# Second head mixing on 64-column halves of TensorE, in a talking-heads attention with a bilinear feed-forward layer

## Chip, core and metric

The kernel runs on one core of one Trainium2 chip. The metric is the device time of one execution in microseconds (us); less is better. All tensors are float32.

## What is computed

```python
def _attn_ref(q, k, v, w_pre, w_post):          # batch 4, 12 heads, 448 positions, 64 per head
    scale = 1.0 / np.sqrt(q.shape[-1])
    scores = scale * np.matmul(q, k.transpose(0, 1, 3, 2))
    scores = np.einsum('bhij,hg->bgij', scores, w_pre)      # first head mixing
    scores = scores - np.max(scores, axis=-1, keepdims=True)
    attn = np.exp(scores)
    attn = attn / (np.sum(attn, axis=-1, keepdims=True) + 1e-09)
    attn = np.einsum('bhij,hg->bgij', attn, w_post)         # second head mixing
    return np.matmul(attn, v).astype(np.float32)

def _moe_ref(x, w_a, w_b, w_out):               # 1792 tokens, 768 wide, 1536 inside
    return ((x @ w_a) * (x @ w_b) @ w_out).astype(np.float32)
```

The reference feeds the attention's output, heads side by side, to the second function.

## The kernel before, in words

Queries are cut into chunks of 120, 120, 120 and 88 per batch, 16 chunks in all, and a chunk into units of 20 queries (`units`, 23 per batch, 92 in all; the last unit of a batch has 8). The loop over `s` (one step per unit) is a software pipeline written out by hand: `tc.manual_schedule()` means that the order in the program is the order on every engine.

In step `s` the program issues, in this order:

- `pace(s - 1)`: a small copy on GpSimd that waits for a row sum of the step before, so that GpSimd's later DMAs don't run ahead;
- `load_v`: pieces of v, issued from GpSimd. Those of batch 0 go out in steps 2 and 4, those of batch b+1 in steps 6 and on of batch b (`V_AT`);
- `premix(s)` (L270): the first head mixing, four small matmuls on four quarters of the array, into the two PSUM buffers of tag `m`;
- `evac_p` of unit s-2 (L314): ScalarE copies the second mixing's result from PSUM to `ptt`;
- `smax(s)` (L279, L280): VectorE's row maximum, then ScalarE's exponential with row sums;
- one `qk` (L233, with its copy by ScalarE on L234) of a chunk that is needed later; its copy writes one of two buffers `s`, so it waits until the gathers of the chunk two before have read that buffer;
- in some steps two `av` (L328), the product with v for a group of eight units;
- `norm(s)` (VectorE: the reciprocal of the sum goes into the small matrix `kr`);
- `postmix` of unit s-1 (L303), the second head mixing, which the change rewrites;
- any second `qk` of the step, and then `load_k`, `load_q` and `spread_q` for later chunks, all on GpSimd (`spread_q` is a copy that `qk` needs).

`gather(u)` (L250) runs three units ahead on SyncE's queue. It is four DMAs of 60 rows of scores, from the buffer `s` into tiles `sb` (four buffers each), so that one unit's rows stand on 60 partitions per five queries.

`postmix` takes a block of ten queries. The probabilities `an` (124 rows: five queries with 12 heads, twice) are the stationary operand, 112 keys at a time, and `kr` (124 x 120) is the moving one. The result has keys on partitions, and four slices of keys side by side:

```python
        for r in range(R):
            nc.tensor.matmul(pp[:, r, :, :n], lhsT=an[:m, r * P:(r + 1) * P], rhs=kr[:m, :, :n])
```

Every float32 matmul shows as two weight loads and two matmuls in the trace, so a unit of two blocks is 16 records of each on L303.

`av` multiplies with v: stationary is v of one head (112 keys x 64), and the two heads of a pair go to the two column halves of the array, to partitions 0 to 63 and 64 to 127 of one PSUM buffer:

```python
                nc.tensor.matmul(
                    xp[64 * e:64 * e + 64, p % 3, :n],
                    lhsT=vt[b, g][:, h % 6, r],
                    rhs=ptt[a][:P, r, h, :n],
```

After the attention come the feed-forward layer's first two products (`run_a`, `run_b`) and the last one (`run_o`). Their PSUM buffers are tags `m` and `p`. `mm3` is three matmuls for every product, since the operands are split in a high and a low part.

The functions that the diff touches, with the profile's line numbers:

Of the kernel before, what the change touches and what calls it, by code (L numbers as in the profile page):

```python
# [7 lines left out]
F32 = mybir.dt.float32  # L8
# [13 lines left out]
def talking_heads_bilinear_kernel(  # L22
# [11 lines left out]
    nc = tc.nc  # L34
    B, _, G, S = k.shape
# [10 lines left out]
    AVC = GU * QU  # L46
    R = 4
    P = S // R
    CW = KD * 128
    AH = 3  # L50
    AV_AT = (1, 1, 3, 3, 5, 5)
# [56 lines left out]
    mask = const.tile([128, QB], F32, name="mask")  # L108
    wp = const.tile([128, 64], F32, name="wp")
    p2 = const.tile([128, 1], F32, name="p2")  # L110

    def ps_t():
        return ps.tile([128, 2, 512], F32, tag="t", name="pst", bufs=1)[:, 0]
# [71 lines left out]

    def load_v(b, i):

        g, e = divmod(i, 3)
        if e == 0:
            vt[b, g] = v_p.tile([P, H // 2, R, D], F32, tag=f"v{g}", name="v")  # L190
        nc.gpsimd.dma_start(out=vt[b, g][:, 2 * e:2 * e + 2], in_=v[b, g][:, 2 * e:2 * e + 2])

    def load_k(b, i):
        t = k_p.tile([128, S], F32, tag="k", name="k")
# [24 lines left out]
    def qk(c, i):  # L219
        b, t0, n = chunks[c]  # L220
        if c not in st:
            st[c] = big.tile([128, H, S], F32, tag="s", name="s")
        if c == 0 and i % 2:
            for g in range(2):
                rows = slice(D * g, D * g + D)
                sp = ps.tile([128, 512], F32, tag="mpx"[i // 2], name="psq")[:, :S]
                nc.tensor.matmul(sp[:n], lhsT=qt[c, i // QG][rows, i % QG], rhs=kt[b, i][rows])
                nc.vector.tensor_copy(st[c][:n, g * G + i], sp[:n])
            return
        sp = ps.tile([128, 2, 512], F32, tag="t", name="pst", bufs=1)[:, :, :S]  # L230
        for g in range(2):
            rows = slice(D * g, D * g + D)
            nc.tensor.matmul(sp[:n, g], lhsT=qt[c, i // QG][rows, i % QG], rhs=kt[b, i][rows])  # L233
        nc.scalar.copy(st[c].rearrange("p (g i) s -> p i g s", g=2)[:n, i], sp[:n])  # L234
# [58 lines left out]
        nc.vector.tensor_scalar(kr[:m], kf[:m], rc[:m], None, op0=ALU.mult)  # L293
        ant[u, j] = a, kr

    def postmix(k_):
        u, j, n = k_
        m = rows_of(n)
        pp = ps.tile([128, 512], F32, tag="p", name="pp")[:P, :R * H * QB]
        pp = pp.rearrange("p (r h t) -> p r h t", r=R, h=H)  # L300
        an, kr = ant.pop((u, j))
        for r in range(R):
            nc.tensor.matmul(pp[:, r, :, :n], lhsT=an[:m, r * P:(r + 1) * P], rhs=kr[:m, :, :n])  # L303
        pps[u, j] = pp

    def evac_p(k_):
        u, j, n = k_
        if (u, j) not in pps:
            return
        a = group_of[u]  # L310
        o = (u - groups[a][1]) * QU + j * QB
        if a not in ptt:
            ptt[a] = big.tile([128, R, H, AVC], F32, tag="pt", name="pt")
        nc.scalar.copy(ptt[a][:P, :, :, o:o + n], pps.pop((u, j))[:, :, :, :n])  # L314

    def av(a, p):
        b, u0, _ = groups[a]
        t0 = (u0 - b * NUB) * QU
        n = min(AVC, S - t0)
        g = p // 3  # L320
        if p % 3 == 0:
            xp = ps.tile([128, 512], F32, tag="x", name="xp")
            xps[g] = xp[:, :3 * AVC].rearrange("p (a t) -> p a t", a=3)
        xp = xps[g]
        for r in range(R):
            for e in range(2):
                h = 2 * p + e
                nc.tensor.matmul(  # L328
                    xp[64 * e:64 * e + 64, p % 3, :n],
                    lhsT=vt[b, g][:, h % 6, r],  # L330
                    rhs=ptt[a][:P, r, h, :n],
                    start=(r == 0),
                    stop=(r == R - 1),
                )
        if p % 3 == 2:
            xs = x_p.tile([128, 3, AVC], F32, tag="xs", name="xs")
            nc.vector.tensor_copy(xs[:, :, :n], xp[:, :, :n])
            later(lambda: nc.sync.dma_start(out=xd[b][:, 3 * g:3 * g + 3, t0:t0 + n], in_=xs[:, :, :n]), 1)
# [127 lines left out]
    def run_b(f, b):  # L466
        hh, ll = wt["f", f]
        x = xt[b]
        pb = (ps_t() if f == b == 0 else ps.tile([128, 512], F32, tag="p", name="pb"))[:, :S]
        mm3(pb, hh, ll, x[:, 0], x[:, 1], KD, KD)  # L470
        sa = sas.pop((f, b))
        hf = w_p.tile([128, S], F32, tag="an", name="hf", bufs=AB)
        nc.vector.tensor_tensor(hf, pb, sa, op=ALU.mult)
        later(lambda: nc.sync.dma_start(out=hd[b][:, f], in_=hf), 1)
# [15 lines left out]
    def run_o(j):  # L490
        b, m = divmod(j, KD)
        hh, ll = wt.pop(("o", j))
        th, tl = ht[b]
        po = ps.tile([128, 512], F32, tag="mp"[j % 2], name="po")[:, :S]
        mm3(po, hh, ll, th, tl, KF)
        so = sb_p.tile([128, S], F32, tag="sb1", name="so")
        nc.scalar.copy(so, po)
# [55 lines left out]
    with tc.manual_schedule():  # L553
# [19 lines left out]
            qk(0, i)  # L573
        spread_q(1, 0)
        setup_w()
        nxt_g = AH + 1
        for u in range(nxt_g):
            gather(u)
# [3 lines left out]
        for s in range(NU + 2):  # L582
# [14 lines left out]
                nxt_g += 1  # L597
            pace(s - 1)
            if s in (2, 4):
                for i in range(3):  # L600
                    load_v(0, 3 * (s // 2 - 1) + i)
            b, i = divmod(s, NUB)
            if b + 1 < B and 0 <= i - V_AT < 6:
                load_v(b + 1, i - V_AT)
            for fn in todo_at.pop(s, ()):
                fn()
# [13 lines left out]
                for k_ in blocks_of(s):  # L620
                    norm(k_)
            if 0 <= s - 1 < NU:
                for k_ in blocks_of(s - 1):
                    postmix(k_)
            for it in pairs[1:]:
                it[0](*it[1:])
            for it in after.get(s, ()):
# [130 lines left out]
```

## Time and profile before

| | |
|---|---|
| time, median of 3 runs | 990.07 us (985.38 to 995.18) |
| span of the profiled execution, first to last instruction | 991.0 us |
| TensorE with a matmul in flight | 963.7 us, 97% of the span |
| VectorE, ScalarE, GpSimd busy | 52%, 42%, 30% |
| attention | to about 466 us; the feed-forward layer from there |
| granted TensorE clock, mean | 0.989 of full speed |

The profiled execution has no separate time of its own; its span of 991.0 us lies 0.9 us above the median and inside the interval of the three runs. Matmuls are pipelined, so a busy TensorE says that something is in flight, not that the array is at its peak. The profile's matmul ends are modelled; the starts are not.

### The profile page before, as it was taken

To read this page: it belongs to the slowest core of one execution; us is meant where nothing else is said; L and a number is where in the kernel's file an instruction comes from. 1 tells how busy PE (TensorE), PEld (TensorE's weight loads), DVE (VectorE), ACT (ScalarE), POOL (GpSimd) and SP (SyncE) were. 2 spreads that over 40 slices of the span, in tenths; PEclk is the share of its full clock that TensorE was granted. 3 is DMA by queue.
4 is the path that set the end of the run, shared out by engine and by line. 5 is a ranking of instruction groups with operands and counts; after the bars stand their busy time and mean duration, and the time that the engine had idled before them with its cause. 6 is when DMAs were issued, how large, how long until landed. Compare 5 with 4: busy or idle time off the path is not lost.

```text
span 991.0 us, 17011 instructions
## 1 busy us (share of the span) xinstructions
PE 963.7 (97%) x6388; PEld 769.2 (78%) x6388; DVE 518.8 (52%) x1096; ACT 415.0 (42%) x851; POOL 292.7 (30%) x321
## 2 busy tenths in 40 slices
PE   8798999999999999989899999999999999999998
PEld 4465566656666666668799999999999989999997
DVE  3355455465555556584876655565665173242500
ACT  3575567676667666653311111111111144243421
POOL 2222012221122111030343332323333045545542
PEclk9899899999999999989999999999999999999999
DMA  4545234543354333374345343433424275637432
GB/s 144 159 152 185 94 130 149 170 150 125 128 175 157 129 115 120 132 229 155 126 131 192 105 145 112 144 113 140 149 93 148 106 272 181 245 127 262 137 124 69
DMA packets 63472, 146.60 MB, mean 148 GB/s; under 512 B 6252, under 2 KB 48000, under 8 KB 62368
## 3 DMA queue, kind: packets, MB, share of 16 engines
q1 hardware_dynamic: 58528, 131.11, 38.5%
q0 software_dynamic: 4864, 14.42, 4.9%
q8 instruction: 51, 0.84, 0.3%
q14 instruction: 29, 0.24, 0.1%
HBM read 80.23 MB, written 26.74 MB: 108 GB/s over the span
## 4 chain that ended last, share of the span: by engine, by line
PE 89%; DVE 3%; DMA 2%; ACT 2%; SPq 1%; issue 1%; POOL 0%; ACTq 0%; DVEq 0%
PE pp L303 15%; PE pst L233 8%; PE mp L270 8%; PE xp L328 8%; PE po L452 6%; PE po L453 6%; PE po L451 6%; PE pa L451 5%; PE pa L452 5%; PE pa L453 5%; PE pb L453 5%; PE pb L451 5%; PE pb L452 5%; DMA sb<-s 1%; ACT s L234 1%; SPq L250 1%
## 5 line engine op out<-in xcount | busy, mean ns | idle before, releaser
L303 PEld LDWEIGHTS pp<-kr,a 124*112 124x112 f32 (+1 forms) x1440 | 155.7, 179 | 48.6 <-issue 25.4
L303 PE MATMUL pp<-kr,a 124*112 124x120 f32 (+1 forms) x1440 | 172.8, 274 | 1.4 <-DVE kr L293 1.1
L279 DVE TENSOR_REDUCE nm<-mp 124x1 f32<-124x448 f32 x180 | 104.2, 619 | 118.3 <-PE mp L270 118.3
L280 ACT ACTIVATE a<-mp,nm 124x448 f32<-124x448 f32 x180 | 112.8, 632 | 87.7 <-DVE nm L279 87.6
L413 POOL TENSOR_TENSOR cvm<-cvm,cvr 128x768 int32<-128x768 int32 x36 | 66.9, 1860 | 211.6 <-DVE cvm L412 211.6
L441 POOL TENSOR_TENSOR wl<-rawo,wh 128x768 fp32r<-128x768 f32 x48 | 93.1, 1960 | 105.9 <-ACT wh L440 105.9
L463 ACT COPY sa<-pa 128x448 f32<-128x448 f32 x48 | 25.7, 536 | 221.6 <-PE pa L453 216.6
L314 ACT COPY pt<-pp 112x480 f32<-112x480 f32 x180 | 96.7, 574 | 45.1 <-PE pp L303 45.0
L121 POOL COPY tick<-rs 60x1 f32<-60x1 f32 x92 | 17.0, 185 | 319.9 <-DVE rs L287 319.9
L233 PE MATMUL pst<-k,q 64*120 64x448 f32 (+1 forms) x372 | 96.8, 598 | 12.2 <-ACT s L234 11.7
L452 PE MATMUL po<-hl,wh 128*128 128x448 f32 x288 | 105.9, 368 | 0.7 <-DVE hl L488 0.7
L452 PE MATMUL pa<-xhl,wh 128*128 128x448 f32 x288 | 104.6, 363 | 1.9 <-DVE xhl L383 1.9
L453 PE MATMUL po<-hh,wl 128*128 128x448 f32 x288 | 105.8, 367 | 0.0
L451 PE MATMUL po<-hh,wh 128*128 128x448 f32 x288 | 105.8, 367 | 0.0
L451 PE MATMUL pa<-xhl,wh 128*128 128x448 f32 x288 | 104.6, 363 | 0.0
L453 PE MATMUL pa<-xhl,wl 128*128 128x448 f32 x288 | 104.4, 363 | 0.0
L453 PE MATMUL pb<-xhl,wl 128*128 128x448 f32 x282 | 102.3, 363 | 0.9 <-POOL wl L441 0.9
L451 PE MATMUL pb<-xhl,wh 128*128 128x448 f32 x282 | 102.2, 362 | 0.0
L452 PE MATMUL pb<-xhl,wh 128*128 128x448 f32 x282 | 102.2, 362 | 0.0
L270 PE MATMUL mp<-sb,wp 60*64 60x448 f32 x720 | 96.9, 571 | 4.6 <-ACT a L280 3.8
L488 DVE TENSOR_TENSOR hl<-hl,hh 128x448 fp32r<-128x448 f32 x48 | 57.5, 1251 | 79.7 <-ACT hh L487 79.7
L234 ACT COPY s<-pst 120x896 f32<-120x896 f32 (+1 forms) x93 | 83.8, 902 | 27.5 <-PE pst L233 14.6
(67 smaller groups left out, 1348.7 us busy)
## 6 DMA issues: line engine op xcount, KB each, us to landing
sb<-s SPq DMA_DIRECT2D x356, 105.0 KB
raw<-in_w_ab_dram SPq DMA_DIRECT2D x24, 768.0 KB
rawo<-wod SPq DMA_DIRECT2D x24, 768.0 KB
hd<-hf SPq DMA_DIRECT2D x48, 224.0 KB
raw<-in_w_out_dram SPq DMA_DIRECT2D x12, 768.0 KB
v<-in_v_dram POOLq DMA_DIRECT2D x24, 224.0 KB, 5.9
xhl<-xd SPq DMA_DIRECT2D x12, 448.0 KB
hl<-hd SPq DMA_DIRECT2D x4, 1344.0 KB
```

The lines of the kernel that those rows point to most:

```text
L233: nc.tensor.matmul(sp[:n, g], lhsT=qt[c, i // QG][rows, i % QG], rhs=kt[b, i][rows])
L234: nc.scalar.copy(st[c].rearrange("p (g i) s -> p i g s", g=2)[:n, i], sp[:n])
L270: nc.tensor.matmul(mt[u, i // 2][col:col + M], lhsT=wp[r:r + m, :M], rhs=tiles[i % 2][r:r + m])
L279: nc.vector.tensor_reduce(nm[:m], mp[:m], axis=AXX, op=ALU.max, negate=True)
L280: nc.scalar.activation(a[:m], mp[:m], ACTF.Exp, bias=nm[:m], scale=1.0, accum_out=rs[:m])
L303: nc.tensor.matmul(pp[:, r, :, :n], lhsT=an[:m, r * P:(r + 1) * P], rhs=kr[:m, :, :n])
L314: nc.scalar.copy(ptt[a][:P, :, :, o:o + n], pps.pop((u, j))[:, :, :, :n])
L328: nc.tensor.matmul(xp[64 * e:64 * e + 64, p % 3, :n], lhsT=vt[b, g][:, h % 6, r], rhs=ptt[a][:P, r, h, :n], start=(r == 0), stop=(r == R - 1),
L441: nc.gpsimd.tensor_tensor(ll[:, sl], raw, hh.bitcast(F32)[:, sl], op=ALU.subtract)
L451: nc.tensor.matmul(o, lhsT=hh[:, k0 + kk], rhs=mh[:, kk], start=(kk == 0), stop=False)
L452: nc.tensor.matmul(o, lhsT=hh[:, k0 + kk], rhs=ml[:, kk], start=False, stop=False)
L453: nc.tensor.matmul(o, lhsT=ll[:, k0 + kk], rhs=mh[:, kk], start=False, stop=(kk == n - 1))
```

## The change

The second head mixing takes keys in slices of 64 (`C`) in place of 112. A block has seven slices. Slice c goes to column half c % 2 of the array and so to partitions 0 to 63 or 64 to 127; the seventh goes to the half that has the block's number (block 0: lower, block 1: upper), and is issued after the first six of both blocks of the unit. The results go to two PSUM tiles, one per block, that are allocated once (`pp_t`) in place of two rotating buffers. The half of the last slot that the seventh slice doesn't write is set to zero once. The copy out of PSUM and `av` take 128 partitions in place of 112.

v is laid out to match: 128 keys per slot, the last slot with its 64 keys in both halves. The array in DRAM stays as it was, so v is now read in pieces of 64 floats (256 bytes) per head and key, where a partition was one run of 2 KB. A slot of six heads takes two DMAs (112 + 16, 96 + 32, 80 + 48 and 64 + 64 rows); a batch has eight slots, hence 16 DMAs in place of six. Batch 0 issues four slots in step 2 and four in step 4; a later batch issues one slot in each of eight steps, where it was one of six pieces in each of six steps.

In the feed-forward layer the buffers that were the rotating pair of tag `p` are named: `p0` and `p1`, by `b % 2` and by `j // 2 % 2`.

```diff
+    C = 64
+    V_PARTS = 4
...
+    pp_t = [ps.tile([128, R, H * QB], F32, tag=f"p{j}", name=f"pp{j}", bufs=1) for j in range(2)]
...
     def load_v(b, i):
 
-        g, e = divmod(i, 3)
-        if e == 0:
-            vt[b, g] = v_p.tile([P, H // 2, R, D], F32, tag=f"v{g}", name="v")
-        nc.gpsimd.dma_start(out=vt[b, g][:, 2 * e:2 * e + 2], in_=v[b, g][:, 2 * e:2 * e + 2])
+        g, slot = divmod(i, V_PARTS)
+        if slot == 0:
+            vt[b, g] = v_p.tile([128, H // 2, R, D], F32, tag=f"v{g}", name="v")
+        runs = [(2 * C * slot, 0, 2 * C)] if slot < R - 1 else [(2 * C * slot, 0, C), (2 * C * slot, C, C)]
+        for s0, p0, n in runs:
+            while n:
+                r, p = divmod(s0, P)
+                m = min(n, P - p)
+                nc.gpsimd.dma_start(out=vt[b, g][p0:p0 + m, :, slot], in_=v[b, g][p:p + m, :, r])
+                s0, p0, n = s0 + m, p0 + m, n - m
...
-                sp = ps.tile([128, 512], F32, tag="mpx"[i // 2], name="psq")[:, :S]
+                if i == 3:
+                    sp = pp_t[g].rearrange("p r c -> p (r c)")[:, :S]
+                else:
+                    sp = ps.tile([128, 512], F32, tag="mx"[i // 4], name="psq")[:, :S]
...
-    def postmix(k_):
-        u, j, n = k_
-        m = rows_of(n)
-        pp = ps.tile([128, 512], F32, tag="p", name="pp")[:P, :R * H * QB]
-        pp = pp.rearrange("p (r h t) -> p r h t", r=R, h=H)
-        an, kr = ant.pop((u, j))
-        for r in range(R):
-            nc.tensor.matmul(pp[:, r, :, :n], lhsT=an[:m, r * P:(r + 1) * P], rhs=kr[:m, :, :n])
-        pps[u, j] = pp
+    def postmix(ks):
+        work = []
+        for u, j, n in ks:
+            an, kr = ant.pop((u, j))
+            pp = pp_t[j].rearrange("p r (h t) -> p r h t", h=H)
+            pps[u, j] = pp
+            m = rows_of(n)
+            for c in range(2 * R - 1):
+                e = c % 2 if c < 2 * R - 2 else j
+                work.append((
+                    c == 2 * R - 2,
+                    pp[C * e:C * e + C, c // 2, :, :n],
+                    an[:m, C * c:C * c + C],
+                    kr[:m, :, :n],
+                ))
+        for late in (False, True):
+            for last, o, lhsT, rhs in work:
+                if last == late:
+                    nc.tensor.matmul(o, lhsT=lhsT, rhs=rhs)
...
-        nc.scalar.copy(ptt[a][:P, :, :, o:o + n], pps.pop((u, j))[:, :, :, :n])
+        nc.scalar.copy(ptt[a][:, :, :, o:o + n], pps.pop((u, j))[:, :, :, :n])
...
-                    rhs=ptt[a][:P, r, h, :n],
+                    rhs=ptt[a][:, r, h, :n],
...
-        pb = (ps_t() if f == b == 0 else ps.tile([128, 512], F32, tag="p", name="pb"))[:, :S]
+        pb = (ps_t() if f == b == 0 else ps.tile([128, 512], F32, tag=f"p{b % 2}", name="pb", bufs=1))[:, :S]
...
-        po = ps.tile([128, 512], F32, tag="mp"[j % 2], name="po")[:, :S]
+        po = ps.tile([128, 512], F32, tag="m" if j % 2 == 0 else f"p{j // 2 % 2}", name="po", bufs=2 if j % 2 == 0 else 1)[:, :S]
...
+        for j in range(2):
+            nc.vector.memset(pp_t[j][C * (1 - j):C * (1 - j) + C, R - 1], 0.0)
...
             if s in (2, 4):
-                for i in range(3):
-                    load_v(0, 3 * (s // 2 - 1) + i)
+                for i in range(V_PARTS):
+                    load_v(0, V_PARTS * (s // 2 - 1) + i)
             b, i = divmod(s, NUB)
-            if b + 1 < B and 0 <= i - V_AT < 6:
+            if b + 1 < B and 0 <= i - V_AT < 2 * V_PARTS:
                 load_v(b + 1, i - V_AT)
...
-                for k_ in blocks_of(s - 1):
-                    postmix(k_)
+                postmix(blocks_of(s - 1))
```

## Rows read from the trace of the kernel before

**Rows 1.** The page's part 4: shares of the chain that ended last, by engine.
```profile
PE 89%; DVE 3%; DMA 2%; ACT 2%; SPq 1%; issue 1%; POOL 0%; ACTq 0%; DVEq 0%
```

**Rows 2.** The chain in order of time: start, length, what (us).
```profile
140.81 1.90 PE xp L328 x32
...
213.74 2.32 PE xp L328 x32
216.06 1.82 PE pp L303 x16
```

**Rows 3.** Groups of weight loads, shapes kept apart: busy us, mean ns, idle before.
```profile
L303 PEld LDWEIGHTS pp<-kr,a 124*112 124x112 f32 x1408 | 152.2, 179 | 45.3 <-issue 23.4 <-ACT pt L314 15.1 <-ACT s L234 3.1
L328 PEld LDWEIGHTS xp<-pt,v 112*64 112x64 f32 x1152 | 72.2, 138 | 23.5 <-issue 17.5 <-ACT pt L314 5.4 <-ACT xhl L382 0.3
```

**Rows 4.** Timeline of weight loads, where the second mixing follows `av`.
```profile
142.63 1.71 PEld L303 LDWEIGHTS pp<-kr,a 124*112 124x112 f32 x16 [0.17 <-issue]
```

**Rows 5.** Stretches, L303 alone: PE, PEld busy (records), clock, DMA share, GB/s.
```profile
0.00:98.00 98.00, 29.93 (x240) 27.11 (x240) 0.97 0.50 160
98.00:163.00 65.00, 24.26 (x200) 21.89 (x200) 0.95 0.35 116
163.00:212.00 49.00, 20.89 (x177) 18.77 (x176) 1.00 0.54 173
212.00:270.00 58.00, 21.86 (x184) 19.63 (x184) 1.00 0.37 124
...
317.00:410.00 93.00, 37.16 (x314) 33.28 (x312) 1.00 0.36 122
410.00:466.00 56.00, 18.04 (x152) 16.22 (x152) 0.94 0.56 184
```

**Rows 6.** Three of these stretches, L328 alone, same columns.
```profile
98.00:163.00 65.00, 13.09 (x192) 11.48 (x192) 0.95 0.35 116
163.00:212.00 49.00, 7.18 (x96) 6.30 (x96) 1.00 0.54 173
...
317.00:410.00 93.00, 20.27 (x288) 17.78 (x288) 1.00 0.36 122
```

**Rows 7.** Timeline of ScalarE: three copies of scores; in brackets idle time before and its releaser.
```profile
41.52 0.91 ACT L234 COPY s<-pst 120x896 f32<-120x896 f32 x1 [5.72 <-DMA sb<-s]
...
98.04 0.91 ACT L234 COPY s<-pst 120x896 f32<-120x896 f32 x1 [2.59 <-DMA sb<-s]
...
283.07 0.90 ACT L234 COPY s<-pst 88x896 f32<-88x896 f32 x1 [0.72 <-issue]
```

**Rows 8.** Timeline of TensorE in two places: first mixings with no `qk` between, and one `qk`.
```profile
33.78 1.02 PE L233 MATMUL pst<-k,q 64*120 64x448 f32 x4 [0.18 <-ACT s L234]
...
416.10 1.46 PE L270 MATMUL mp<-sb,wp 60*64 60x448 f32 x8
...
419.31 1.05 PE L270 MATMUL mp<-sb,wp 60*64 60x448 f32 x5
```

**Rows 9.** Timeline of ScalarE: the second copy out of the second mixing, and the next exponential.
```profile
217.92 0.57 ACT L314 COPY pt<-pp 112x480 f32<-112x480 f32 x1 [0.26 <-PE pp L303]
219.64 0.64 ACT L280 ACTIVATE a<-mp,nm 124x448 f32<-124x448 f32 x1 [1.15 <-DVE nm L279]
```

**Rows 10.** Parts 3 and 6 of the page: GpSimd's DMA queue (packets, MB, share), and v's issues.
```profile
q0 software_dynamic: 4864, 14.42, 4.9%
...
v<-in_v_dram POOLq DMA_DIRECT2D x24, 224.0 KB, 5.9
```

**Rows 11.** Timeline of GpSimd at the start.
```profile
1.47 1.41 POOL L132 DMA_DIRECT2D wrep<-in_w_pre_dram  x2 [0.95 <-DVE p L144]
...
25.95 1.63 POOL L191 DMA_DIRECT2D v<-in_v_dram  x3 [0.32 <-issue]
...
28.16 0.83 POOL L211 COPY q<-qraw 128x360 f32<-128x360 f32 x1
```

**Rows 12.** Timeline of VectorE: one product after `run_b`.
```profile
491.08 0.62 DVE L473 TENSOR_TENSOR hf<-pb,sa 128x448 f32<-128x448 f32 x1 [0.40 <-PE pb L453]
```

## The prediction, made before the changed kernel ran

> **What bounds the kernel now.** I read the chain of waits first. TensorE is 89% of it [rows 1], so a change that takes TensorE time off can pay; the reader should then ask where this share isn't true. The chain in order of time prices the runs of matmuls: a run of L303 (16 records) is 1.82 us, a run of two `av` (32 records) 2.32 us with 160 columns and 1.90 us with 128 [rows 2]. An undisturbed step with one `qk` is first mixing, `qk`, second mixing, some 3.7 us, and some 6 us with `av`.
>
> Next come stretches of the attention with their DMA share. It is 0.35 to 0.37 in the stretches 98 to 163, 212 to 270 and 317 to 410 us, but 0.50 before 98 and 0.54 from 163 to 212 [rows 5] (270 to 317 repeats the latter, with as many units). Then the copies of scores on ScalarE, which must wait until older scores have been gathered: at 41.52 one waited 5.72 us for the gathers' DMA, at 98.04 one 2.59 us, and at 283.07 one 0.72 us in a stretch where TensorE still looks full [rows 7]. So in the busy stretches the gathers are the bound (before 98 us) or stand right behind TensorE (163 to 212, 270 to 317). Only the quiet stretches are TensorE's alone.
>
> **The change part by part.** *Slices of 64 in pairs.* `av` already sends two heads to the two column halves, so its rows price a pair. From 160 to 128 columns a run of 16 pairs of records falls by 0.42 us, 26 ns per pair for 32 columns, 0.82 ns per column [rows 2]. With 120 columns 16 pairs would take 1.90 - 16 x 8 x 0.00082 = 1.80 us: what 16 single records of L303 take today (1.82). A pair costs as much as a single. If a pair is proportional to its columns it takes 105 ns at 128 and 98 ns at 120, and the run carries 1.90 - 16 x 0.105 = 0.22 us of filling and draining. A full unit now has 14 matmuls, 28 records, 14 pairs: 0.22 + 14 x 0.098 = 1.60 us, 0.22 saved. Bounds: if records can't be issued faster than in the 128-column run, 14 x 0.105 + 0.22 = 1.69, 0.13 saved; the shorter weight load at the head of a run (138 against 179 ns [rows 3]) gives 0.04 more at best. I take 0.22. The last unit of a batch has one block, whose seventh slice has no partner; I count nothing for it.
>
> The weight loads must hide for this, and in `av` they do: of 1.90 / 16 = 119 ns per pair 105 go with the columns, which leaves 14 ns for two loads of 138 ns [rows 2, 3]. The Trainium skill speaks against it ("TensorE: Matmul & The Clock Gate", Part 3, The mechanism): a weight load overlaps matmuls in flight only when its row group differs, and both halves here use the same rows. By that rule every pair would stand for its loads, which these rows of `av` don't show.
>
> *No change of tiling after `av`.* The second mixing now uses the same column tiling as `av`, which precedes it in `av` steps. Today the weight loads stand still for 0.17 us there with no wait to name [rows 4], and the first load must fill. I take 0.19 us per `av` step, bounds 0 and 0.22 (the whole fixed part). The changes to the first mixing and from `qk` remain.
>
> *What of this is kept.* Units (records / 16) and `av` steps (records / 32) are: 98 to 163, 12 full and 6; 212 to 270, 11 and again 6; 317 to 410, 19 and 9 [rows 5, 6]. Savings there: 12 x 0.22 + 6 x 0.19 = 3.8, then 3.6, then 5.9: 13.3 us. Each busy middle stretch has 11 units and 3 `av` steps, 3.0 us [rows 5, 6]; since copies late in it wait for gathers already and those early in it don't, I keep a quarter, 1.5 for both. Before 98 us (15 units, 3.3 us) I keep nothing: the copy at 98.04 waits for DMA whatever TensorE does. After 410 us (9.5 units, 2.1 us) the feed-forward layer's loads are in the way, DMA share 0.56 [rows 5]; nothing. Together 14.8 us.
>
> *Would something else hold the step?* A step of 3.47 us must still cover first mixing, maximum, exponential and the freeing of PSUM. The shortest step in the trace, 419.31 - 416.10 = 3.21 us [rows 8], shows that this fits, with 0.26 us to spare. Both copies out of PSUM now start when the whole unit is done, not one at its middle: 2 x 0.57 us from 217.7 or so end at 218.9, before the next exponential at 219.64 [rows 9]. Nothing is queued behind them but that exponential, so this is free; without that cover it costs at most 0.57 us a step.
>
> *v in pieces of 256 bytes, DMA side.* GpSimd's queue took 4.9% of 16 engines' 991 us, 777 engine-us for 14.42 MB [rows 10]: 3.4 us per MB if spread evenly. v is 24 x 224 KB, 5.5 MB: 4.6 us per batch. The new layout reads 8/7 of the bytes: 5.3 us, 0.7 more, if cost goes by bytes. At the other end, each piece as an average packet (777 / 4864 = 160 ns): 6144 pieces per batch / 16 x 160 ns = 61 us. But the packets hold 3.0 KB on average [rows 10], more than one run of v: runs share packets. I stay near the first row and take 1 us per batch. It falls where gathers bind: two batches before 98 us, one in each busy middle stretch: 4 us.
>
> The Trainium skill ("DMA: Bandwidth & Descriptors", Why small descriptors are slow) puts a 256-byte packet at 11 cycles, 27% of them overhead; an estimate by that page is 5.3 / 0.73 = 7.3 us of v, 2.7 us more per batch rather than 1, and a time some 7 us higher. No run here shows it yet.
>
> *v, GpSimd side.* Issuing three pieces of v took 1.63 us, 0.54 each, for 112 rows; two small DMAs of 60 rows took 1.41 us, 0.70 each [rows 11]. Between 60 and 112 rows nothing grows, so I take 0.54 per DMA however many pieces. Step 2 then holds GpSimd 8 x 0.54 = 4.3 us in place of 1.6. Queued behind are a load of q and the copy of q at 28.16, done by 31.7 instead; its `qk` starts at 33.78 [rows 8, 11]. Free. In later steps a second 0.54 us DMA fits. The dear end (0.54 us per 112 pieces) is a rival.
>
> *The rest.* Two small memsets come before VectorE's first reduction; the waits for gathers before 98 us swallow them. In the feed-forward layer some neighbouring `run_b` get the same buffer; VectorE reads it as soon as it is done (it waited 0.40 us for TensorE [rows 12]), while a whole `run_a` of 18 matmuls runs between. Free, unless VectorE falls over 3 us behind.
>
> Sum: 14.8 - 4 = 10.8 us, 991.0 - 10.8 = 980.2 for the span; 0.9 less against the median: 979.
>
> **Rivals.** *Gathers don't bind.* For it: TensorE's busy share and the chain [rows 1]. Against: the waits and shares [rows 5, 7]. Then 13.3 + 6.0 + 3.3 + 2.1 = 24.7 us are kept: 965 to 967.
>
> *v's pieces cost the DMA engines half again as much.* For: they are an eighth of today's runs. Against: shared packets. 4.6 x 1.15 x 1.5 = 7.9 us, 3.3 more per batch, 13 us in all: 988. Double would be 24 us and 999; from 3.7 us per batch on the change loses.
>
> *GpSimd's issue goes by descriptors* (the slower side). 0.54 / 112 = 4.8 ns per piece, 3.7 us per slot of 768. Step 2 then holds GpSimd for 14.8 us, the copy of q at 28.16 ends at 42, and `qk` of 33.78 stands until then with both mixings queued behind it on TensorE. The wait until 41.52 hides part [rows 7, 8, 11]; some 4 us are lost, some 6 in step 4, and about 1 us in each of three batches, where 4 us of issue meet steps of 4.8 us on average: 13 us, 992. At the 11.7 ns per row of the two small DMAs a slot takes 9 us, twice a step, and the time passes 1050. It decides from some 4 ns per piece.
>
> *The pairs don't run side by side.* If the halves' records came one after the other a unit would be 28 singles, 0.22 + 28 x 0.098 = 2.96 us, 1.1 us more for 89 units: 1090. The `av` rows speak against it.
>
> **How the numbers follow.** One per cent, 9.9 us, is what a measurement of this kernel can tell from no change. Forecast 0.54 (972 to 985; 0.34 of it beyond 1% faster, 0.20 within), gathers free 0.18 (faster), dear DMA pieces 0.15 (0.11 within, 0.04 slower), dear issue 0.11 (0.04 and 0.07), no pairs 0.02. Faster 0.52, same 0.35, slower 0.13. The range, 965 to 994, reaches from the second case through the third and the cheap half of the fourth; the sum's own bounds (0.13 us for a unit, 0.7 us for v) lie in it.
>
> **What would show it.** Right: runs of 28 records on the second mixing in 1.6 us; quiet steps shorter by 0.2 us, and by 0.4 with `av`; longer waits of the score copies for gathers in the busy stretches, and the end of the first stretch not before 98 us; GpSimd's issues of v near 0.54 us. Wrong: issues of v of 2 us and more, waits of `qk` for the copies of q, `av` waiting for v, or the busy stretches shrinking as much as the quiet ones.

## The result, and the profile after

The changed kernel takes 994.84 us (median of 20 runs, 992.34 to 1001.79) against 987.75 (20 runs, 984.28 to 995.18): 1.0075 of the time before, 95% interval 1.0057 to 1.0092. Forecast were 979 and a range of 965 to 994. The profiled execution took 994.76 us with a span of 993.1. Of the runs below, two of ten of b_vpieces_at4 (1003 and 1005 us) and one of ten of b_vpieces8 (1006) were in a slower state and are left out of their medians.

One thing has to come off before the traces are compared. In the profiled execution of before, the matmuls of the feed-forward layer's last product follow each other 206.7 ns apart, in that of after 200.0 ns, as the timelines of TensorE show (before, then after; start, length). From the first to the second line there are 40 and 41 such steps.

```profile
859.68 0.37 PE L453 MATMUL po<-hh,wl 128*128 128x448 f32 x1
...
867.95 0.37 PE L451 MATMUL po<-hh,wh 128*128 128x448 f32 x1
```

```profile
859.68 0.36 PE L476 MATMUL po<-hh,wl 128*128 128x448 f32 x1
...
867.88 0.36 PE L475 MATMUL po<-hl,wh 128*128 128x448 f32 x1
```

Over 864 records that is 5.8 us of before's span. Three of the twenty profiled executions of this study have it, with either mixing, so it isn't the change's. I therefore compare by the attention: the first mixing of its last unit starts at 448.09 us before and at 455.12 after, 7.0 us later, as the medians say (7.1).

TensorE's own steps became what was forecast. The timeline of an undisturbed step, before and then after:

```profile
122.34 0.98 PE L270 MATMUL mp<-sb,wp 60*64 60x448 f32 x8
...
126.02 0.98 PE L270 MATMUL mp<-sb,wp 60*64 60x448 f32 x8
```

```profile
126.44 0.98 PE L283 MATMUL mp<-sb,wp 60*64 60x448 f32 x8
127.35 1.02 PE L246 MATMUL pst<-k,q 64*120 64x448 f32 x4
128.30 1.66 PE L327 MATMUL pp<-kr,a 124*64 124x120 f32 x28
129.88 0.98 PE L283 MATMUL mp<-sb,wp 60*64 60x448 f32 x8
```

The 28 records of the second mixing take 1.58 us from their start to that of the next instruction, and the step takes 3.44 us (3.68 before). After `av` they take less. In the chain of waits [rows 2] has 2.32 us for `av` and 1.82 for the second mixing; after has

```profile
131.81 2.32 PE xp L351 x32
134.13 1.44 PE pp L327 x28
```

The weight loads are shorter and 28 per unit in place of 16 (groups, shapes apart; [rows 3] has 179 ns):

```profile
L327 PEld LDWEIGHTS pp<-kr,a 124*64 124x64 f32 x2464 | 130.5, 138 | 38.1 <-ACT pt L337 25.1 <-issue 11.1 <-ACT a L293 1.3
```

What stands between such steps is in the timeline of ScalarE: the copies of scores that waited for gathers, to be held against [rows 7]. Here are four of them.

```profile
46.72 0.91 ACT L247 COPY s<-pst 120x896 f32<-120x896 f32 x1 [10.54 <-DMA sb<-s]
...
73.70 0.90 ACT L247 COPY s<-pst 88x896 f32<-88x896 f32 x1 [4.61 <-DMA sb<-s]
...
104.22 0.91 ACT L247 COPY s<-pst 120x896 f32<-120x896 f32 x1 [4.24 <-DMA sb<-s]
...
213.92 0.91 ACT L247 COPY s<-pst 120x896 f32<-120x896 f32 x1 [8.17 <-DMA xd<-xs]
```

A fifth stands at 323.42 (7.92 us), and two shorter ones, of 3.05 and 3.29 us, at 181.10 and 290.82. In the kernel before, the copy in the place of the one at 213.92 didn't wait, and neither did that in the place of 323.42 (at 311.32):

```profile
206.06 0.91 ACT L234 COPY s<-pst 120x896 f32<-120x896 f32 x1
```

The copies at 213.92 and 323.42 name another DMA, which is only the last of several that they wait for; the chain of waits goes to the gathers (SPq is SyncE's issue of one):

```profile
181.07 8.62 DMA sb<-s
189.70 13.52 DMA sb<-s
203.24 0.74 SPq L263
204.04 9.66 DMA sb<-s
213.92 0.92 ACT s L247
```

An issue takes SyncE 0.74 us; by this chain 8.6 to 13.5 us pass from a gather's issue to what its landing releases. SyncE, too, waits for earlier gathers before it can issue the next. Its waits for them in all (before, then after; us in total, times, longest) more than doubled:

```profile
SPq L250 <- DMA sb<-s: 16.2, 30, 1.7
```

```profile
SPq L263 <- DMA sb<-s: 36.5, 53, 1.8
```

The DMA share of the busy stretches, by contrast, hardly rose: it is 0.57 and 0.56 (0.54 in [rows 5]), and GpSimd's queue holds 5.5% (4.9 in [rows 10]). Below are the stretches with L327 alone (the DMA share is the last number but one), and the queue's line on the page:

```profile
163.00:212.00 49.00, 18.02 (x308) 15.95 (x308) 0.97 0.57 169
270.00:317.00 47.00, 18.02 (x308) 16.01 (x308) 1.00 0.56 167
```

```profile
q0 software_dynamic: 6016, 15.21, 5.5%
```

On the page TensorE's share of the chain fell from 89% [rows 1] to 76%, and that of DMA rose from 2% to 14%:

```profile
PE 76%; DMA 14%; DVE 3%; ACT 2%; SPq 1%; issue 1%; POOL 0%; ACTq 0%; DVEq 0%
```

And a wait costs more than itself. Here is TensorE's timeline at the copy of 213.92, and below it three stretches: the wait, what follows it, and the next 5.6 us. The granted clock is the last number but two of each line.

```profile
205.11 1.66 PE L327 MATMUL pp<-kr,a 124*64 124x120 f32 x28
214.88 1.85 PE L246 MATMUL pst<-k,q 64*120 64x448 f32 x4 [8.11 <-ACT s L247]
216.66 1.77 PE L283 MATMUL mp<-sb,wp 60*64 60x448 f32 x8
218.36 1.35 PE L246 MATMUL pst<-k,q 64*120 64x448 f32 x4
```

```profile
206.80:214.80 8.00, 0.00 (x0) 0.00 (x0) 0.00 (x0) 0.88 (x1) 1.00 (x2) 0.63 0.54 170
214.80:219.60 4.80, 4.72 (x16) 1.25 (x16) 1.07 (x2) 2.19 (x5) 0.00 (x0) 0.55 0.34 126
219.60:225.20 5.60, 5.60 (x74) 4.04 (x74) 3.54 (x15) 4.88 (x12) 0.36 (x2) 1.00 0.31 108
```

After 8 us without a matmul the granted clock is 0.55, near the lower level of 1.2 GHz: `qk` takes 1.85 us in place of 1.02, the first mixing 1.77 in place of 0.98, the next `qk` 1.35 in place of 1.02: 1.95 us more in all.

By the starts of first mixings the account closes. Places are those in the trace of before, and a plus is time lost: 0.4 us at 16.01; +4.7 from there to 106.64; -5.5 to 202.94; +9.8 in the two steps from there; -5.2 to 308.11; +9.3 in the two steps from there; -6.5 to 448.09; together +7.0. By the stretches of [rows 5] the quiet ones saved 3.5, 3.5 and 5.9 us, the busy ones lost 7.8 and 7.6, and the first lost 4.7.

### The profile page after: what moved, and what is told of

Same layout as the page of the kernel before. It is cut to its first block, busy times and chain, and to the rows that moved or that the text cites. A ratio compares the mean times of both kernels' runs of the same rounds, so it can differ in the third digit from the quotient of the medians.

```text
span 993.1 us, 19213 instructions
## 1 busy us (share of the span) xinstructions
PE 938.4 (95%) x7468; PEld 748.4 (75%) x7468; DVE 524.3 (53%) x1098; ACT 411.1 (41%) x851; POOL 321.5 (32%) x361
## 3 DMA queue, kind: packets, MB, share of 16 engines
q0 software_dynamic: 6016, 15.21, 5.5%
## 4 chain that ended last, share of the span: by engine, by line
PE 76%; DMA 14%; DVE 3%; ACT 2%; SPq 1%; issue 1%; POOL 0%; ACTq 0%; DVEq 0%
DMA sb<-s 11%; PE pp L327 9%; PE pst L246 6%; PE mp L283 6%; PE po L475 6%; PE po L476 6%; PE po L474 6%; PE pa L474 5%; PE pa L475 5%; PE pa L476 5%; PE pb L476 5%; PE pb L475 5%; PE pb L474 5%; PE xp L351 5%; DMA xd<-xs 2%; SPq L263 1%
## 5 line engine op out<-in xcount | busy, mean ns | idle before, releaser
L327 PEld LDWEIGHTS pp<-kr,a 124*64 124x64 f32 (+1 forms) x2520 | 133.2, 138 | 42.0 <-ACT pt L337 28.3
L327 PE MATMUL pp<-kr,a 124*64 124x120 f32 (+1 forms) x2520 | 150.0, 271 | 1.8 <-DVE kr L306 1.7
L337 ACT COPY pt<-pp 128x480 f32<-128x480 f32 x180 | 93.1, 574 | 46.3 <-PE pp L327 46.3
L283 PE MATMUL mp<-sb,wp 60*64 60x448 f32 x720 | 102.1, 581 | 6.4 <-ACT a L293 4.8
L246 PEld LDWEIGHTS pst<-k,q 64*120 64x120 f32 (+1 forms) x372 | 26.9, 179 | 102.4 <-ACT s L247 59.4
```

The source lines that it names most:

```text
L283: nc.tensor.matmul(mt[u, i // 2][col:col + M], lhsT=wp[r:r + m, :M], rhs=tiles[i % 2][r:r + m])
L327: nc.tensor.matmul(o, lhsT=lhsT, rhs=rhs)
L337: nc.scalar.copy(ptt[a][:, :, :, o:o + n], pps.pop((u, j))[:, :, :, :n])
```

## Experiments

A change of buffer is the step of a batch (3, 9, 15 and 20) from which score copies write a buffer `s` whose last gathers were issued one step earlier. The gathers must be done by then.

The theories of where the time went:

- A: v's later slots go out beside the loads of k, which begin in step 12, just ahead of a change of buffer.
- B: v in pieces of 256 bytes takes more from the gathers than its bytes.
- C: faster steps alone leave the same transfers too little time.
- D, which came later: gathers are delivered at a pace of their own, and v in steps 6 to 15 of a batch takes its share of it.

| second mixing | v | us | ratio to before, 95% | last first mixing, us |
|---|---|---|---|---|
| old | before: whole, steps 6 to 11 | 987.75 | | 448.09 |
| new | the change: pieces, 6 to 13 | 994.84 | 1.0057 to 1.0092 | 455.12 |
| old | b_vpieces: pieces, 6 to 13 | 995.25 | 1.0064 to 1.0110 | 455.19 |
| new | a_vhost: whole, 6 to 11 | 983.88 | 0.9945 to 0.9993 | 438.90 |
| new | a_vat4: pieces, 4 to 11 | 986.83 | 0.9985 to 1.0022 | 444.50 |
| new | a_vspread: the same, first batch spread | 989.24 | 0.9997 to 1.0033 | 444.66 |
| old | b_vat8: whole, 8 to 13 | 992.02 | 1.0038 to 1.0077 | 450.87 |
| old | b_vpieces_at4: pieces, 4 to 11 | 990.9 | 1.0002 to 1.0065 | 454.41 |
| old | b_vpieces8: pieces, 8 DMAs, 6 to 11 | 994.47 | 1.0039 to 1.0107 | 455.25 |
| old | b_vtwice: whole, 12 DMAs, 6 to 11 | 987.59 | 0.9974 to 1.0033 | 448.61 |
| old | b_v8sbuf: pieces in DRAM only | 998.18 | 1.0088 to 1.0153 | 455.80 |
| old | b_v8dram: pieces in SBUF only | 995.96 | 1.0057 to 1.0123 | 457.73 |
| old | b_v8both: the same slots, whole | 985.58 | 0.9981 to 1.0015 | 446.02 |
| old | b_vquiet: whole, 17 to 22 | 980.39 | 0.9897 to 0.9968 | 441.22 |
| new | a_vquiet: pieces, 17 to 22, 0 and 1 | 974.79 | 0.9837 to 0.9933 | 437.73 |
| new | a_vquiet15: pieces, 15 to 22 | 978.39 | 0.9823 to 0.9940 | 432.85 |
| new | a_vquiet_spread: a_vquiet, first batch spread | 972.96 | 0.9831 to 0.9898 | 434.75 |
| new | a_vhost_quiet: whole, 17 to 22 | 963.62 | 0.9739 to 0.9804 | 425.66 |
| new | a_ah4: the change, gathers 4 ahead | 988.78 | 1.0000 to 1.0042 | 453.76 |
| new | a_vquiet_ah4: a_vquiet, gathers 4 ahead | 973.77 | 0.9855 to 0.9917 | 434.55 |

Steps are those of a batch (0 to 22). Before's median in the sets was 987.1 to 989.0. Whole v for the new mixing keeps the rows that are read twice, an eighth of what is read. The last column is from the one profiled execution of each kernel, which can lie some 5 us from the median (a_vhost's took 978.56), so small differences in it decide nothing.

**The parts of the change, apart.** b_vpieces has the old matmuls and the change's traffic: pieces of the same length, 16 DMAs per batch and the same steps, but no rows read twice (14.42 MB on GpSimd's queue against 15.21).

```diff
-        nc.gpsimd.dma_start(out=vt[b, g][:, 2 * e:2 * e + 2], in_=v[b, g][:, 2 * e:2 * e + 2])
+        for p0, p1 in ((0, 96), (96, P)):
+            nc.gpsimd.dma_start(out=vt[b, g][p0:p1, :, r], in_=v[b, g][p0:p1, :, r])
```

> The kernel before with its old second mixing, but v read in 256-byte pieces by 16 DMAs per batch (rows 0 to 95 and 96 to 111 of each slot), four slots in each of steps 2 and 4 and eight slots in steps 6 to 13. Theories A and B: steps of the old speed stall as well where v meets the loads of k; some 5 to 9 us at each of two places and up to 6 in the first 17 units, 998 to 1010. Theory C: at the old speed the gathers keep up, 987 to 991.

995.25, between the two expectations: the traffic alone costs 8 us, and the whole change is no slower than that. The stalls in the busy stretches are where the change has them, but shorter (ScalarE's timeline):

```profile
209.54 0.91 ACT L235 COPY s<-pst 120x896 f32<-120x896 f32 x1 [2.50 <-DMA sb<-s]
...
318.82 0.91 ACT L235 COPY s<-pst 120x896 f32<-120x896 f32 x1 [2.64 <-DMA sb<-s]
```

a_vhost has the new mixing without pieces; the host writes v in slots of 128 keys:

```diff
+    rows = _np.concatenate([_np.arange(384), _np.arange(384, 448), _np.arange(384, 448)])
-        "v": v.reshape(B, 2, H // 2, 4, S // 4, D).transpose(0, 1, 4, 2, 3, 5),
+        "v": v.reshape(B, 2, H // 2, S, D)[:, :, :, rows].reshape(B, 2, H // 2, 4, 128, D).transpose(0, 1, 4, 2, 3, 5),
```

> The changed kernel, but with v in the new order already in DRAM, so that six DMAs per batch read 128 partitions in runs of 2 KB, in the steps of the kernel before: the second mixing alone is changed. Theories A and B: no stalls of 9 us and no loss in the first 17 units, the forecast's 14.8 us and something of the busy stretches are kept: 965 to 975. Theory C: the stalls stay, 990 to 995.

983.88, between the two: of TensorE's saving some 3 us arrive (1 to 5 by the interval). Of the two long stalls one stays, with v as large runs and no overlap with k. Others came at earlier changes of buffer: 6.00 us at 69.92 and 4.35 at 279.75. And this is the trace of the fastest of its ten runs.

```profile
201.69 0.91 ACT L241 COPY s<-pst 120x896 f32<-120x896 f32 x1 [5.09 <-DMA sb<-s]
```

In this trace the two busy stretches lost 4.3 and 3.5 us where the forecast had a saving, without any pieces. So C holds in part, and so does B or A.

**Moving v's slots by two steps.** a_vat4 is the change with `V_AT = 4`; b_vat8 is before with `V_AT = 8`; b_vpieces_at4 is b_vpieces with 4.

> The changed kernel with the eight slots of v for the next batch two steps earlier (steps 4 to 11 of a batch in place of 6 to 13), so that the last two no longer go out beside the loads of k, which begin at step 12. Theory A (the slots meet the loads of k in the DMA engines just before the gathers of units 40 and 63): both stalls, some 9 us each, go back to what they were, about 977 us. Theory B (small pieces take DMA time wherever they lie): the stalls shrink by half at most, 985 to 992. Theory C (the faster steps alone bring the same loads too close before the gathers): 993 to 996, no difference from the changed kernel.

986.83. The two stalls of some 9 us went, but of these 18 us only 8 were gained, because other waits grew at the change of buffer before them, where the slots now end (3.05 and 3.29 us there in the change):

```profile
181.50 0.90 ACT L247 COPY s<-pst 88x896 f32<-88x896 f32 x1 [6.40 <-DMA sb<-s]
...
287.28 0.90 ACT L247 COPY s<-pst 88x896 f32<-88x896 f32 x1 [6.07 <-DMA sb<-s]
```

> The kernel before with its six DMAs of v, in runs of 2 KB, two steps later (steps 8 to 13 of a batch in place of 6 to 11), so that the last two go out beside the loads of k as in the change, but whole. Theory A (the meeting with k): stalls as with the small pieces at the same place, 993 to 996. Theory B (the pieces): 987 to 989. Theory D (gathers are delivered at a pace of their own through steps 6 to 15, and each byte of v there takes its share, whenever in it): the same bytes with two steps less to recover, 988 to 992.

> The kernel before with v in 256-byte pieces, eight slots, in steps 4 to 11 in place of 6 to 13, so that none meets the loads of k. Theory A: 987 to 989. Theory B: 993 to 996, as in steps 6 to 13. Theory D: between, 988 to 992, with a wait of the score copy at the earlier change of buffer (step 10 of a batch) as well.

992.02 and 990.9: at the old speed whole runs that meet the loads of k, and pieces that don't, cost some 4 to 5 us each by the medians, in D's range or at its edge. The traces have the last first mixing 2.8 and 6.3 us later, so which of the two costs more isn't settled. Neither A nor B by itself explains both.

a_vspread also sends the first batch's slots one per step:

```diff
-            if s in (2, 4):
-                for i in range(V_PARTS):
-                    load_v(0, V_PARTS * (s // 2 - 1) + i)
+            if 2 <= s < 2 + 2 * V_PARTS:
+                load_v(0, s - 2)
```

> As the first kernel of this set, and the eight slots of v for the first batch go out one per step in steps 2 to 9 in place of four in each of steps 2 and 4. Theory A: the first 17 units lose about 2 us in place of 6, so some 4 us less than the first kernel, about 973. Theory B: the same bytes in the same stretch, no more than 1 us less than the first kernel. Theory C: as the first kernel within 1 us, since gathers there are behind whatever v does.

989.24, nothing gained: the first wait shrank (from 9.42 us in a_vat4 to 4.64), but with the next batch's v from step 4 on a longer one came at the following change of buffer (a step of 12.18 us at 68.45). With v of later batches out of the way (a_vquiet_spread below) it may be some help.

**v out of the busy stretches.** The slots go where DMA is least busy:

```diff
-    V_AT = 6
+    V_AT = 17
...
-            b, i = divmod(s, NUB)
-            if b + 1 < B and 0 <= i - V_AT < 2 * V_PARTS:
-                load_v(b + 1, i - V_AT)
+            b, i = divmod(s - V_AT, NUB)
+            if 0 <= b < B - 1 and i < 2 * V_PARTS:
+                load_v(b + 1, i)
```

> The changed kernel with the eight slots of v for batch b+1 in steps 17 to 22 of batch b and 0 and 1 of batch b+1, where DMA is least busy, in place of steps 6 to 13. Theory A, widened (whatever v puts beside the loads of k and q just ahead of a change of buffer stalls the score copies, in its place): no stall above 2 us at the steps of 202 and 312 us, the first 17 units lose 4 us less, no new stall: 968 to 974. Theory B (pieces cost wherever they lie): 980 to 988. Theory C (the faster steps alone, with the loads of k and q): no better than the kernel whose v was laid out in DRAM, 981 to 986.

> The kernel before with its six DMAs of v per batch in steps 17 to 22 in place of 6 to 11, nothing else. Theory A, widened: the old steps had little to lose, 2 to 4 us in the first 17 units: 983 to 986. Theories B and C: 986 to 988.

974.79 and 980.39. Even the kernel before gains 7 us, where I expected 2 to 4: its wait at 98.04 [rows 7] is gone, and only one score copy waits for gathers (5.9 us at 41). With the new mixing the stalls near 202 and 312 us are gone, but pieces bring waits into the quiet steps. TensorE's timeline there shows one, ahead of a second mixing that takes 1.66 us elsewhere; the granted clock from 150 to 153 us was 0.50:

```profile
149.04 1.02 PE L246 MATMUL pst<-k,q 64*120 64x448 f32 x4 [2.00 <-ACT s L247]
149.99 3.07 PE L327 MATMUL pp<-kr,a 124*64 124x120 f32 x28
```

> The second mixing alone changed (v lies in DRAM in the new order, six DMAs of 2 KB runs per batch) and v in the quiet steps 17 to 22. Theory A: the quiet steps take pieces and whole runs alike, 970 to 973, better only by the first steps. Theories B and D: the three waits of 1.7 us that the pieces bring into the quiet steps go too, 965 to 969.

963.62, below every expectation: new mixing, whole runs, quiet steps. Against b_vquiet the new mixing is worth 16.8 us (15.6 by the last first mixing); the same kernel with v in steps 6 to 11 is 20 us slower. This one beats both the kernel before and the change.

> The changed kernel with v of later batches in the quiet steps, and the eight slots of the first batch one per step in steps 2 to 9 in place of four in each of steps 2 and 4. By A, B and D alike the wait of 10.4 us at the step of 36 us comes from the eight slots ahead of it; spread, it falls to the 5.9 us of the kernel before or less: 969 to 972. If those gathers are late for another reason, 974 to 976.

> The changed kernel with its pieces of v in steps 15 to 22 of a batch, so that no slot lies in steps 0 and 1, two steps ahead of the change of buffer in step 3. If the waits of some 3.4 us per batch in the kernel with slots in steps 17 to 22, 0 and 1 came from where the last slots lay: they go, 964 to 968. If pieces cost wherever they are: they stay or move to the change of buffer in step 20, 972 to 976.

a_vquiet_spread took 972.96, between the two expected ranges and too near a_vquiet for the noise. In its trace the wait of 10.40 us in the first batch fell to 2.40 (then for TensorE), but one of 7.02 us came at 67.78.

a_vquiet15 took 978.39. Its profiled execution (978.27) has the 206.7 ns in the last product; without those 5.8 us it would be some 972. Whether its other runs have them isn't known; one took 971.92. Ending the slots earlier shrank the waits at the change of buffer of step 3 (from some 4.1 us to 2.93 and less) and brought others at that of step 20 (2.87 us at 121.06). Pieces cost in the quiet steps too: against a_vhost_quiet the last first mixing is 7 us later here, and 12 us later in a_vquiet.

**More cover.** Gathers go four units ahead, and the copies start two steps behind the last gather of the buffer in place of one. To make room the probabilities have four buffers (`AB`) in place of five, which wasn't tried by itself.

```diff
-    AB = 5
+    AB = 4
...
-    AH = 3
+    AH = 4
...
-        a, e = max(starts[c - 1] - AH, 0), starts[c] - AH
+        a, e = max(starts[c - 1] - AH + 1, 0), starts[c] - AH
```

> The changed kernel with gathers four units ahead in place of three (five buffers of each tile of gathered rows) and the products of a chunk beginning one step later after the last gathers that read their buffer, two steps in place of one; four buffers of probabilities in place of five to make room. If the stalls are this wait of the copy for the last gathers of the chunk two before, a whole step of 3.4 to 5.6 us more covers them: both 9 us stalls fall to 4 to 5, 982 to 986 by theories A and B, and by C as well. If the gathers are simply too slow for the TensorE in these stretches, the wait moves to the first mixing and the time stays at 992 to 996.

988.78, between the two expectations and no gain on before. The two steps fell from 14.07 and 13.86 us to 9.27 and 9.15, as expected, but other waits grew (the step at 94 takes 12.27 us, 10.16 in the change). With v in the quiet steps as well (a_vquiet_ah4):

> The first and the third kernel of this set together. Theory A, widened: 964 to 970, the forecast's 14.8 us and most of what the busy stretches could give. Theories B and C: 975 to 982.

973.77, a miss: 1 us less than a_vquiet, which the noise can hold. In a_vquiet no score copy in the two busy stretches waits over 1.12 us, so there was little left to cover.

**What in the pieces costs.** b_vpieces8 loads a slot of 112 rows in one DMA, in the steps of before; b_vtwice cuts the DMAs of before in halves of 56 rows:

```diff
+        nc.gpsimd.dma_start(out=vt[b, g][:, :, r], in_=v[b, g][:, :, r])
```

```diff
+        for p0, p1 in ((0, 56), (56, P)):
+            nc.gpsimd.dma_start(out=vt[b, g][p0:p1, 2 * e:2 * e + 2], in_=v[b, g][p0:p1, 2 * e:2 * e + 2])
```

> The kernel before with v in 256-byte pieces, but as one DMA per slot of 112 rows (8 per batch), in steps 6 to 11 of a batch as before (two slots in the first and the fourth of these steps). If the length of the pieces costs: 991 to 993, some 4 us, as with 16 DMAs in steps 4 to 11. If the number of DMAs or the steps cost: 986 to 989.

> The kernel before with each DMA of v cut in two of 56 rows: 12 per batch, runs of 2 KB as before, in the steps of before. If the number of DMAs costs: 990 to 993. If only the length of the pieces or the steps: 986 to 989.

994.47 and 987.59: it is the length of the runs, not the number of DMAs. And pieces in the steps of before, away from the loads of k, cost nearly what they cost in steps 6 to 13 (995.25).

The last three have the slots of b_vpieces8 and differ in which side is scattered: with the first line a slot lies together in SBUF (b_v8sbuf), with the second in DRAM (b_v8dram), with both on both sides (b_v8both).

```diff
+            vt[b, g] = v_p.tile([P, R, H // 2, D], F32, tag=f"v{g}", name="v")
+        "v": v.reshape(B, 2, H // 2, 4, S // 4, D).transpose(0, 1, 4, 3, 2, 5),
```

> As the kernel before with one DMA of pieces per slot, but a slot of six heads lies together in SBUF (1.5 KB per partition), so that only the DRAM side is in pieces of 256 bytes. If the scattered reads cost: 993 to 996, as with pieces on both sides. If the scattered writes cost: 986 to 989.

> The same with a slot of six heads together in DRAM (1.5 KB per partition) and in pieces of 256 bytes in SBUF. If the scattered reads cost: 986 to 989. If the scattered writes cost, or a descriptor for every piece whichever side it is on: 993 to 996.

> The same slots in the same steps with runs of 1.5 KB on both sides. If it is the pieces: 986 to 989. If it is two slots in one step: 991 to 996.

998.18, 995.96 and 985.58: against whole slots, 256 bytes on either side cost 10 to 13 us; runs of 1.5 KB on both sides cost nothing. SyncE's waits for earlier gathers follow (pieces in DRAM only, pieces in SBUF only, whole runs):

```profile
SPq L250 <- DMA sb<-s: 26.9, 43, 1.8
```

```profile
SPq L250 <- DMA sb<-s: 31.0, 52, 2.0
```

```profile
SPq L250 <- DMA sb<-s: 11.6, 20, 1.6
```

The pages show how little of it stands in GpSimd's own queue; pieces in DRAM only, then whole runs:

```profile
q0 software_dynamic: 4992, 14.42, 5.3%
```

```profile
q0 software_dynamic: 4992, 14.42, 5.0%
```

The difference, 0.3% of 16 engines' 990 us, is 3 us of the span if spread evenly. GpSimd's issue grows a little, for a slot 784 ns against 546 (groups of its instructions, same order):

```profile
L191 POOL DMA_DIRECT2D v<-in_v_dram x32 | 25.0, 784 | 7.0 <-issue 6.2 <-PE pp L303 0.8
```

```profile
L191 POOL DMA_DIRECT2D v<-in_v_dram x32 | 17.4, 546 | 6.0 <-issue 5.3 <-PE pp L303 0.7
```

## Why the prediction was wrong, step by step

*Pairs, and no change of tiling after `av`: right.* A unit's second mixing takes 1.58 us (1.60 forecast), a short step lost 0.24 us (0.22), a step with `av` 0.39, 0.15 more (0.19). The weight loads hide: L327's 2520 take 138 ns each, 3.9 us for 28, and 28 records take 1.58 us. The rule that the prediction quoted against it doesn't show here. The mechanism was right here, and the quiet stretches saved 12.9 us of the 13.3 that the sum had for them.

*What of this is kept: wrong, and the step that failed.* What failed is "Each busy middle stretch has 11 units and 3 `av` steps, 3.0 us [...] I keep a quarter". I let a busy stretch take back at most what it saves itself. The two gave back 9.8 and 9.3 us, savings of the quiet stretch ahead of them included. A copy follows the last gather of its buffer by one step; each step before it gives the gathers 0.24 to 0.39 us less, while the transfers stay, and the wait at the end brings the lower clock with it.

In place of the 14.8 us the new mixing is worth 0.4 us with the change's v (b_vpieces against the change), which is nothing clear of noise, some 3 us with v as before and 16.8 with v in the quiet steps. A gain of 10.8 us was forecast and a loss of 7.1 measured, 17.9 us apart: some 14 of them are this step, and some 4 the traffic below.

The 16.8 us lie near the 14.8 partly by luck. By first mixings that kernel saved 10.8 us in the quiet stretches (13.3 forecast), 4.6 in the two busy ones (1.5) and 2.0 in the first (none), and lost 1.7 at the end of the attention.

*"I keep nothing: the copy at 98.04 waits for DMA whatever TensorE does": wrong.* That wait came from where v's transfers lay and not from the gathers alone: b_vquiet hasn't got it. And the stretch can lose: 4.7 us, with waits for gathers of 10.54, 4.61 and 4.24 us where before had 5.72 and 2.59 [rows 7].

*v in pieces, DMA side: mis-sized.* I took 1 us per batch, 4 in all; at the old speed the traffic costs 8. Pieces cost some 4 us in steps 4 to 11 and 5 to 13 in steps 6 to 11, without meeting the loads of k. That meeting, which I hadn't priced at all, costs some 5 with whole runs; with pieces it adds nothing clear of the noise, so the two don't simply add. "It falls where gathers bind" was right, but I priced it by the queue's time and not by the gathers'. By the queue's share the pieces cost some 3 us, near my sum by bytes; the loss is in the gathers. The rival of half again to double the DMA time (988 to 999) has the measured time in its range, but not its reason, since the queue's time didn't grow by half. The Trainium skill ("DMA: Bandwidth & Descriptors", Why small descriptors are slow) gave, as an estimate, 2.7 us more per batch, 10.8 in all. That includes the rows read twice; without them the same estimate is 4.6 / 0.73 - 4.6 = 1.7 us per batch, 6.8 in all. At the old speed, without such rows, pieces on both sides cost 5 to 8 us (b_vpieces8, b_vpieces) and pieces on one side 10 to 13, so the size agrees roughly. The Trainium skill puts this on the DMA engines' own time per packet, and the share above shows 3 us of it; where the rest is lost no row shows.

*GpSimd's issue: right in kind.* A DMA of v takes 664 ns to issue on average (0.54 us forecast), and step 2 holds GpSimd as below, 5.25 us in place of the forecast 4.3. The `qk` behind the copy of q waited 0.18 us for it, as long as it waited for ScalarE before [rows 8]. By the two slot kernels 560 runs more cost 238 ns of issue, 0.4 ns each, not 4.8: the rival of issue by descriptors falls.

```profile
26.39 5.25 POOL L200 DMA_DIRECT2D v<-in_v_dram  x8 [0.36 <-issue]
32.67 0.57 POOL L212 DMA_DIRECT2D qraw<-in_q_dram  x1 [1.03 <-DMA v<-in_v_dram]
```

*Step cover, copies, memsets, named buffers: right.* Undisturbed steps hold at 3.44 us, and the feed-forward layer takes 538 us from the last first mixing to the end, as it does with the old mixing (537 in b_vquiet). The 3.21 us of the cover argument aren't the shortest step of before: the one from 413.37 to 416.10 takes 2.74 us, which only widens the cover.

*What would show it.* The signs of being right came true and none of the signs of being wrong did, while the time was wrong: "longer waits of the score copies for gathers" stood among the former, with no size. A sign that both outcomes share tells nothing.

Open: why 256-byte pieces hold the gathers back by more than the time of their own packets. That they do is shown by the slot kernels; how, isn't, and the pace of theory D wasn't measured by itself. The same page of the Trainium skill (Queues, rings and completion order) says that an engine takes the queues in turn, a packet at a time; no view here shows that order.

## What to carry to other kernels

A saving on the busiest engine is worth what the transfers with a deadline leave of it: look for the shortest distance between a transfer's issue and the instruction that reuses its buffer, and price what is queued beside it there, before adding up the quiet stretches. A new layout that shortens the runs of a DMA on either side should be paid for by a layout in DRAM that keeps them whole; moving the transfers to steps in which less is due helps as well, but here pieces still cost some 9 us there. Placing a prefetch by hand deserves its own experiment: here the steps in which v goes out were worth 7 us to the old kernel and 20 to the new.

## What the runs showed of the hardware

- After 8 us without a matmul TensorE's granted clock was 0.55 over the next 4.8 us, and its work there took 2 us more (the change, from 206.8 us). In a_vquiet, after a pause of 2.00 us and one `qk`, a second mixing took 3.07 us in place of 1.66, at a granted clock of 0.50 from 150 to 153 us.
- The two column halves run side by side on the same rows with different weights: 14 pairs of records take 1.58 us, where 16 single ones took 1.82, and 28 weight loads of 138 ns each, 3.9 us in all, hide in that time.
- Pieces of 256 bytes cost as much on the SBUF side alone (995.96 us) as on the DRAM side alone (998.18; 985.58 with whole runs on both). GpSimd's queue grew from 5.0% to 5.3% by them, and SyncE's waits for earlier gathers from 11.6 us to 31.0 and 26.9.
- Cutting the same runs of 2 KB into twice as many DMAs cost nothing (987.59 us against 989.0), and 560 more pieces in a DMA cost GpSimd's issue 238 ns.
- In three of the twenty profiled executions (before, b_vtwice, a_vquiet15) the last product's records stood 206.7 ns apart from start to start, in the others 200.0, at a granted clock of 1.00 in both; what differs isn't known.
